# Six early output stores issued by ScalarE, SyncE's loads in the order of use, and two stretches of attention moved up by 14 products

## The chip, the cores and the metric

The kernel runs on one core of a Trainium2 chip. Times are device microseconds (us) of one execution, given as the median of several with the range; most executions of one kernel agree within 0.3%. A difference counts as faster or slower where it is over 2%.

## The reference, cut to what matters

```python
# q, k, v: (8 batches, 8 heads, 576 positions, 64)   all float32
scores = q @ k^T / 8
ret    = scores * Dmat            # Dmat[h,i,j] = gamma_h ** (i-j) for i >= j, else 0
x      = (ret @ v) as (4608 tokens, 512)
out    = ((x @ w_a) * (x @ w_b)) @ w_out      # 512 -> 1536 -> 512
```

A retention (attention without a softmax, whose decay allows running states) feeds a gated feed-forward network. Nearly all arithmetic is in the three products of the network.

## The kernel before

The 4608 tokens are handled as 18 pairs of 128. TensorE runs the network block by block: 512 tokens, 256, 256, then 512 each. Between its products stand the pieces of attention for later tokens. The first six 128-row steps use small pieces (transposing on TensorE, scores, states, outputs); from pair 3 on a whole pair is done in one "stretch" whose transposed queries and keys come from DMA transposes.

SyncE issues the loads, the transposes and the stores, all in one list, in the order of the program text as the build's scheduler lays it out:

```python
def load_pair(n, which=(0, 1, 2)):          # q, k, v of one pair, two issues each
    paired.setdefault(n, [])
    for i in which:
        ...
        for kp, r0, m, b, s0 in rows_of(n):
            nc.sync.dma_start(t[...], src[b, :, s0:s0 + m, :]...)
        paired[n].append(t)

def turn(n):                                 # q and k of a pair, transposed by DMA
    for w in (0, 1):
        nc.sync.dma_start_transpose(qkT[:, w]..., qkb[:, w])

def store(u, cols, osb):                     # one 128-token output tile
    ...
    if n < FIRST:                            # FIRST = 3: the first six tiles
        for par in (0, 1):                   # their tokens are interleaved: two half stores
            nc.sync.dma_start(rows[par::2], osb[half(par), cols])
    else:
        nc.sync.dma_start(rows, osb[r0:r0 + m, cols])
```

ScalarE and VectorE evict. Three of ScalarE's copies matter here: the transposed queries of the small steps, the running states, and `ha`, the first of the two activations, which frees one of four PSUM buffers:

```python
COPY["act"](qkT[:, w], tp...)               # line 318, before score_step
nc.scalar.copy(ha[:, 0:n], pa[:, 0:n])      # line 690, once per 128 columns of w_a
...
if (u + part) % 2 == 0:                      # an output tile leaves PSUM
    nc.scalar.copy(osb[:, cols], po[:, 0:width])
else:
    nc.vector.tensor_copy(osb[:, cols], po[:, 0:width])
store(tok0 // 128 + u, cols, osb)            # osb has four buffers
```

A table says at which count of products each piece is laid into the stream:

```python
todo += [(170, stretch, (3, None)), (197, stretch, (4, 3)),
         (246, stretch, (5, 4)), (280, stretch, (6, 5)), ...]
casts = {3: 104, 4: 104.1, 5: 143, 6: 200, 7: 250, 8: 330}
turns = {4: 104.2, 5: 151, 6: 210, 7: 338, 8: 345}
loads = {7: 212, 8: 271, 9: 345.1, 10: 345.2}
```

`stretch(6, 5)` scores pair 6 and finishes pair 5. Synchronization is not written by hand: the framework gives each transfer of SyncE and ScalarE one of eight completion counters in turn, and makes the issuer wait until the previous user of that counter has landed.

## Time and profile before

| | before |
|---|---|
| median time (4 runs) | 333.47 us (332.73 to 334.26) |
| span of the profiled execution | 331.8 us |
| TensorE busy | 319.8 us, with 36 of its 3648 matmul records missing |
| ScalarE busy | 128.6 us (39%) |
| mean granted TensorE clock | 1.00 |

The prediction below shows the page's busy times, the chain, the waits and the time line; they are not repeated. Two rows from the table of windows of before serve for comparison later. They give, for each stretch of time, every engine's busy microseconds, then the granted clock, the mean share of the DMA engines that is busy, and the traffic.

```profile
core 0: us, PE busy (x) PEld busy (x) DVE busy (x) ACT busy (x) POOL busy (x), PEclk, DMA share, GB/s
40.00:60.00 20.00, 19.63 (x221) 12.61 (x223) 9.49 (x17) 8.63 (x22) 14.83 (x20) 1.00 1.04 225
60.00:80.00 20.00, 18.47 (x322) 14.13 (x322) 12.94 (x29) 9.66 (x24) 10.12 (x12) 1.00 1.08 205
```

TensorE has work for 38.1 of these 40 us, ScalarE for 18.3, and the DMA engines are full.

One reading needs care. Before's list of waits has ten of 0.16 us each at the output products and six at the first products "until issue". They are 1.6 and 1.0 us, and I take them for missing records: runs 9 and 10 below, which also have 3612 matmul records, have the same entries, and the kernels with all 3648 have not. So TensorE's true busy time is about 319.8 + 2.6 = 322.4 us (an estimate), to be used when it is compared with kernels whose records are complete.

### The profile page before, as it was taken

What the parts mean: (1) busy time and instruction counts of PE and PEld (TensorE: products, weight loads), DVE (VectorE), ACT (ScalarE), POOL (GpSimd) and SP (SyncE); (2) the same over time, 40 slices, a digit from 0 to 9 for tenths busy, and PEclk for the clock granted to TensorE, in tenths of its full rate; (3) what the DMA queues carried; (4) which work ended last, traced back from release to release, by engine and by line L of the source; (5) the groups of instructions that cost most, each with busy time, mean ns of one, the idle gap of its engine ahead of it and who ended that gap; (6) DMA issues with size and microseconds to landing.
All of it is one profiled execution on the core that took longest, in us unless ns stands there. A gap on an engine that the chain in (4) does not pass through costs nothing.

```text
span 331.8 us, 8671 instructions
## 1 busy us (share of the span) xinstructions
PE 319.8 (96%) x3612; PEld 168.1 (51%) x3648; DVE 163.7 (49%) x292; ACT 128.6 (39%) x275; POOL 114.6 (35%) x146
## 2 busy tenths in 40 slices
PE   8999999989989999999999999999999999999996
PEld 4644456848634554545454545454445444444443
DVE  5734435664674465656265625662456246414321
ACT  7734744553543344343235313532332333213321
POOL 4870078835277274634063405360430000000000
DMA  8999999999999998992599258945850420031013
GB/s 220 248 172 208 236 227 222 225 166 234 199 205 254 214 215 200 206 219 54 140 224 213 61 127 188 224 71 149 180 116 4 138 54 0 2 95 34 1 26 100
DMA packets 143175, 50.37 MB, mean 152 GB/s; under 512 B 124576, under 2 KB 138656, under 8 KB 143136
## 3 DMA queue, kind: packets, MB, share of 16 engines
q1 hardware_dynamic: 138384, 45.10, 65.0%
q0 software_dynamic: 4752, 4.72, 8.7%
q8 instruction: 28, 0.46, 0.6%
q14 instruction: 11, 0.09, 0.1%
HBM read 37.75 MB, written 9.44 MB: 142 GB/s over the span
## 4 chain that ended last, share of the span: by engine, by line
PE 86%; DMA 5%; SPq 2%; issue 2%; DVE 2%; ACT 1%; POOL 1%; DVEq 0%; POOLq 0%; ACTq 0%
PE po L716 27%; PE pb L697 27%; PE pa L682 26%; SPq L153 2%; DMA vf<-in_v_dram 2%; DMA qf<-in_q_dram 2%; PE o L589 2%; PE o L602 1%; DMA qkT<-qkb 1%; PE sc L563 1%; PE kv L506 1%; PE kv L359 1%; DVE sums L526 0%; POOL qkb L440 0%; PE pa L664 0%
## 5 line engine op out<-in xcount | busy, mean ns | idle before, releaser
L702 DVE TENSOR_TENSOR hT<-ha,pb 128x512 bf16<-128x512 bf16 (+1 forms) x120 | 75.8, 633 | 99.6 <-PE pb L697 95.2
L690 ACT CAST ha<-pa 128x512 bf16<-128x512 f32 (+1 forms) x120 | 64.8, 543 | 122.7 <-PE pa L682 121.5
L697 PE MATMUL pb<-xT,wb_sb 128*128 128x512 bf16 (+1 forms) x474 | 111.5, 357 | 0.4
L682 PE MATMUL pa<-xT,wa_sb 128*128 128x512 bf16 (+1 forms) x459 | 108.4, 357 | 2.8 <-DVE xT L612 1.4
L716 PE MATMUL po<-wo_sb,hT 128*128 128x512 bf16 (+1 forms) x430 | 95.0, 373 | 1.8 <-issue 1.6
L697 PEld LDWEIGHTS <-wb_sb 128*128 128x128 bf16 x480 | 46.8, 98 | 46.4 <-issue 0.3
L682 PEld LDWEIGHTS <-wa_sb 128*128 128x128 bf16 x474 | 45.5, 98 | 46.7 <-issue 1.9
L716 PEld LDWEIGHTS <-hT 128*128 128x128 bf16 x444 | 42.3, 98 | 46.8
L440 POOL CAST qkb<-qf 64x1024 bf16<-64x1024 f32 x15 | 15.4, 1029 | 85.8 <-DMA qf<-in_q_dram 85.0
L445 POOL TENSOR_TENSOR vb<-vf,vs 128x1024 bf16<-128x1024 f32 x15 | 28.5, 1901 | 12.4 <-DMA vf<-in_v_dram 6.3
L727 DVE COPY osb<-po 128x512 f32<-128x512 f32 (+1 forms) x18 | 12.2, 676 | 40.7 <-PE po L716 40.7
L725 ACT COPY osb<-po 128x512 f32<-128x512 f32 (+1 forms) x19 | 10.9, 574 | 44.4 <-PE po L716 41.5
L526 DVE TENSOR_TENSOR sums<-kv,sums 128x256 f32<-128x256 f32 x46 | 19.5, 423 | 2.8 <-PE kv L506 0.8
L612 DVE TENSOR_TENSOR xT<-o,qs 128x512 bf16<-128x512 f32 x30 | 19.6, 682 | 2.5 <-PE o L602 2.5
L572 DVE TENSOR_TENSOR sT<-sc,mask 128x512 bf16<-128x512 f32 x30 | 19.4, 680 | 0.0
L444 POOL CAST qkb<-kf 64x512 bf16<-64x512 f32 x30 | 17.6, 614 | 0.9
L444 POOL CAST qkb<-qf 64x512 bf16<-64x512 f32 x30 | 17.6, 614 | 0.7
L440 POOL CAST qkb<-kf 64x1024 bf16<-64x1024 f32 x15 | 15.5, 1033 | 4.2 <-DMA kf<-in_k_dram 3.2
L530 ACT CAST states<-sums 64x512 bf16<-64x512 f32 x26 | 16.0, 617 | 0.3
L299 POOL CAST qkb<-kf 128x512 bf16<-128x512 f32 x5 | 3.1, 613 | 20.0 <-DMA kf<-in_k_dram 20.0
L740 PE MATMUL w<-ones 128*128 128x256 bf16 (+1 forms) x36 | 8.3, 359 | 1.5 <-DVE ones L197 1.5
L563 PE MATMUL sc<-qkT 64*64 64x64 bf16 x480 | 7.4, 195 | 1.3 <-DMA qkT<-qkb 1.3
(81 smaller groups left out, 155.7 us busy)
## 6 DMA issues: line engine op xcount, KB each, us to landing
qf<-in_q_dram SPq DMA_DIRECT2D x32, 256.0 KB, 4.5
kf<-in_k_dram SPq DMA_DIRECT2D x32, 256.0 KB, 5.1
vf<-in_v_dram SPq DMA_DIRECT2D x32, 256.0 KB, 5.1
out_dram<-osb SPq DMA_DIRECT2D x25, 256.0 KB, 2.2
out_dram<-osb SPq DMA_DIRECT2D x22, 128.0 KB, 2.4
wo_sb<-in_moe_w_out_dram POOLq DMA_DIRECT2D x3, 512.0 KB, 18.0
qf<-in_q_dram SPq DMA_DIRECT2D x8, 128.0 KB, 3.2
kf<-in_k_dram SPq DMA_DIRECT2D x8, 128.0 KB, 3.5
```

What stands on the lines that cost most here:

```text
L440: nc.gpsimd.tensor_copy(qkb[0:64, w], t[0:64])
L444: nc.gpsimd.tensor_copy(to[:, :, 1 - r], fro[:, :, r])
L445: nc.gpsimd.tensor_tensor(vb.rearrange("p (k h d) -> p k h d", k=2, h=H), vf.rearrange("p (k h d) -> p k h d", k=2, h=H), vs2[:, 2 if n in ...
L526: nc.vector.tensor_tensor(sums[:, i], own, prev, op=ALU.add)
L530: nc.scalar.copy(to(half(1 - r)), fro(half(r)))
L572: nc.vector.tensor_tensor(sT[:, on].rearrange("p c k s -> p (c k) s"), sc[:, on].rearrange("p c k s -> p (c k) s"), mask3.unsqueeze(1).to_ ...
L612: nc.vector.tensor_tensor(x_of(t0, 128).rearrange("p c (a s) -> p c a s", a=2), o[:, :, :, kp].rearrange("p a c s -> p c a s"), qs[:, :, s ...
L682: nc.tensor.matmul(pa[:, 0:n], wa_sb[:, c, fs], xT[:, c], start=(c == 0), stop=(c == NC - 1))
L690: nc.scalar.copy(ha[:, 0:n], pa[:, 0:n])
L697: nc.tensor.matmul(pb[:, 0:n], wb_sb[:, c, fs], xT[:, c], start=(c == 0), stop=(c == NC - 1))
L702: nc.vector.tensor_tensor(hT[:, F, 0:n], has[F][:, 0:n], pb[:, 0:n], op=ALU.mult)
L716: nc.tensor.matmul(po[:, 0:width], hT[:, F, u * 128:(u + 1) * 128], wo_sb[:, F, cols], start=(F == 0), stop=(F == NF - 1))
```

## The change

The intent: the first output tile is ready at 43 us, and its store stands in SyncE's list behind loads that move at the pace of the transfers. Let ScalarE issue the first six tiles' stores; close up SyncE's loads and transposes for pairs 4 to 7 in the order of use; with the transposes earlier, lay two stretches 14 products earlier so that their results are there before the next block wants them. (The 14 is the table's count, and a piece is laid in at the next edge of a group of products: in the traces the first stretch moves up by 32 products of half the width, that is 16, and the second by 12.) In the 256-token blocks both output tiles are evicted by ScalarE, so that the issuer of the store is also the engine that made the tile.

```diff
             if n < FIRST:
                 for par in (0, 1):
-                    nc.sync.dma_start(rows[par::2], osb[half(par), cols])
+                    nc.scalar.dma_start(rows[par::2], osb[half(par), cols])
...
-                if (u + part) % 2 == 0:
+                if n == 256 or (u + part) % 2 == 0:
                     nc.scalar.copy(osb[:, cols], po[:, 0:width])
...
-    for n in range(FIRST, FIRST + 3):
+    for n in (FIRST, FIRST + 1):
         load_pair(n)
+    load_pair(FIRST + 2, (Q, K))
...
-             (246, stretch, (5, 4)), (280, stretch, (6, 5)),
+             (232, stretch, (5, 4)), (266, stretch, (6, 5)),
...
-    casts = {3: 104, 4: 104.1, 5: 143, 6: 200, 7: 250, 8: 330}
-    turns = {4: 104.2, 5: 151, 6: 210, 7: 338, 8: 345}
-    loads = {7: 212, 8: 271, 9: 345.1, 10: 345.2}
-    todo += [(150, load_pair, (6, (0, 1))), (152, load_pair, (6, (2,)))]
+    casts = {3: 104, 4: 104.1, 5: 141, 6: 200, 7: 250, 8: 330}
+    turns = {4: 104.2, 5: 142, 6: 213, 7: 338, 8: 345}
+    loads = {7: 146, 8: 271, 9: 345.1, 10: 345.2}
+    todo += [(104.3, load_pair, (5, (V,))), (104.4, load_pair, (6, (K,))),
+             (112.2, load_pair, (6, (Q,))), (112.4, load_pair, (6, (V,)))]
```

Cut from the diff: `paired[n]` becomes a dictionary, so that single tensors of a pair can be loaded at different places.

More of the change, by code (lines that the diff above doesn't have):

```diff
@@ L136, in load_pair @@
             return
-        paired.setdefault(n, [])
+        paired.setdefault(n, {})
         for i in which:
@@ L145, in load_pair @@
                     src[b, :, s0:s0 + m, :].rearrange("h s d -> s h d"))
-            paired[n].append(t)
+            paired[n][i] = t
     def load_step(n, hh, which):
@@ L433, in ahead @@
     def ahead(n):
-        qf, kf, vf = paired.pop(n)
+        qf, kf, vf = (paired[n].pop(i) for i in (Q, K, V))
         qkb = nat.tile([128, 2, 2 * DM], BF16, tag="qkb", name="qkb2")
```

## The prediction

> **What bounds the kernel now.** I read the page's first and fourth parts, then the waits of TensorE, then the time line of TensorE, ScalarE and SyncE between 34 and 76 us, where all the moved instructions stand.
>
> ```profile
> PE 319.8 (96%) x3612; PEld 168.1 (51%) x3648; DVE 163.7 (49%) x292; ACT 128.6 (39%) x275; POOL 114.6 (35%) x146
> PE 86%; DMA 5%; SPq 2%; issue 2%; DVE 2%; ACT 1%; POOL 1%; DVEq 0%; POOLq 0%; ACTq 0%
> PE pa L682 <- DVE xT L612: 1.4, 1, 1.4
> PE sc L563 <- DMA qkT<-qkb: 1.3, 1, 1.3
> ```
>
> TensorE sets the end: 96% busy, 86% of the chain. Its list of waits has only two that this change can remove: 1.3 us for the transposed pair 4 (at 70 us) and 1.4 us for the last activations of the fourth token block (at 95 us). With the small holes that lengthen four product groups between 82.7 and 86.8 us to 4.1 us from some 3.5, the whole prize is 3.3 us, 1%.
>
> Next, SyncE, whose rows are start, length, what it issues:
>
> ```profile
> 34.91 0.65 SPq L806 DMA_DIRECT2D gate<-wo_sb  x1
> ...
> 45.81 2.75 SPq L142 DMA_DIRECT2D vf<-in_v_dram x2
> 48.68 2.35 SPq L142 DMA_DIRECT2D qf<-in_q_dram x2
> ...
> 55.20 2.29 SPq L142 DMA_DIRECT2D qf<-in_q_dram x2
> 57.59 3.38 SPq L142 DMA_DIRECT2D kf<-in_k_dram x2
> 61.07 1.87 SPq L142 DMA_DIRECT2D vf<-in_v_dram x2
> 63.04 1.46 SPq L653 DMA_DIRECT2D out_dram<-osb x2
> 64.60 3.28 SPq L471 DMA_TRANSPOSE qkT<-qkb x2
> 67.97 3.88 SPq L653 DMA_DIRECT2D out_dram<-osb x6
> ```
>
> SyncE is held at a gate until the output weights have landed (34.9 us); then it issues loads back to back, about 1.15 us for each 256 KB, which is the 220 to 227 GB/s of the page's slices there: it goes at the pace of the transfers. So the first store leaves at 63.0 us. Against that, the engines:
>
> ```profile
> 42.58 0.59 ACT L725 COPY osb<-po 128x512 f32<-128x512 f32 x1 [0.38 <-PE po L716]
> 43.67 0.59 ACT L318 COPY qkT<-tp 128x512 bf16<-128x512 bf16 x1 [0.50 <-PE tp L316]
> 44.65 0.42 PE L331 MATMUL sc<-qkT 64*64 64x128 bf16 x16
> 48.63 0.42 PE L331 MATMUL sc<-qkT 64*64 64x128 bf16 x16
> ```
>
> The first output tile is ready at 43.2 us and waits 20 us in SyncE's queue. Right behind it ScalarE copies the transposed queries that TensorE needs at 44.65 us.
>
> **What the Trainium skill says.** "DMA: Bandwidth & Descriptors", section "Issuing engines are not separate DMA queues": transfers issued by SyncE and ScalarE share the same 16 DMA engines, and issuing from two saves only issue time. The trace agrees so far that one queue moves 65% of 16 engines' time and the loads are paced by transfer. "Perfetto Trace Analysis", section "DMA Instruction — HWDGE (DVE, Sync)": the sequencer itself sits in the semaphore wait before such an issue, and the profiler's row starts after it. The trace has such a case: the gate's row starts at 34.91 us, and none of the loads listed behind it, which wait for nothing that the weights give, goes before it. The trace of before has no DMA on ScalarE; that ScalarE's queue blocks alike is my inference.
>
> **The change, part by part.** (1) Twelve half stores (six tiles, two issues each) leave SyncE's list and stand in ScalarE's. In the trace eight of them take 546 to 819 ns each, median 597, to issue: 12 x 0.6 = 7.2 us of ScalarE, which is 39% busy; by itself nearly hidden. (2) In the two 256-token blocks both output evictions go to ScalarE: two more copies of 0.59 us, two fewer of 0.69 on VectorE. Hidden. (3) SyncE's loads and transposes for pairs 4 to 7 close up by the eight half stores' 5.3 us or so; transposed pair 4 is there long before its use. (4) Two stretches stand 14 products earlier. TensorE's work is the same in number (7298 rows in both programs).
>
> But the built program says what a store waits for, beside its tile. All transfers of SyncE and ScalarE take eight completion counters in turn, in one common order, and each waits for the one before it on its counter. In that common order the stores are interleaved with loads that SyncE has not reached in reality, since the gate and the transfers hold it back. ScalarE works strictly down its list, so it will stand at the store until that load has landed, and the query copy behind it stands too. I walk down the six tiles, with issue times and landing times from the trace of before (SyncE's list is unchanged up to the k of pair 5):
>
> Tile 1, first half: waits for the second half of pair 3's v, issued 46.65, landed 5.8 us later: 52.4. Second half: second half of pair 4's q, issued 49.5 + 4.7 = 54.2. Issue 0.7, query copy 0.6: TensorE's first score step moves from 44.65 to 55.5, +10.9.
> Tile 2: second half of pair 5's q (56.2 + 6.1 = 62.3), then first half of its k (57.6 + 5.6 = 63.2). Issue 0.7, copy 0.6: the second score step moves from 48.63 to 64.5, +15.9. The work between the two steps, 4 us, disappears inside this wait.
> Tile 3: second transpose of pair 4, then first half of pair 5's v. SyncE is through with k at 61.0, transposes take 1.4 + 1.8, so v leaves at 64.2 and lands a median 4.7 later: 68.9. Issue 0.7, state copy 0.5: the second output step moves from 52.74 to 70.1, +17.4.
> Tile 4: first half of pair 6's q, four loads of 1.1 us behind that v: 68.6 + 4.7 = 73.3. Issue 0.7, copy of a 0.4: TensorE, which has four PSUM buffers for products and so runs two product pairs ahead, gets its third at 74.4 instead of 55.91, +18.5.
> Tile 5 (block 1, first half): first k and v of pair 7; by then SyncE is ahead: no wait.
> Tile 6: second transpose of pair 6, then q of pair 8. That transpose waits for TensorE to have read pair 3's queries (its first stretch with states, 68.6 before, so 87.1). Two transposes 3.2 (90.3), q lands 4.5 later (94.8), issue and copy 1.0: 95.8 for the third product of block 2, 75.99 before. Without this wait it would come at 75.99 + 18.5 - 1.3 (the wait for pair 4, now gone) = 93.2; so 2.6 more, +19.8.
>
> From there TensorE is dense (192.1 of the 195 us from 105 to 300 us busy, by the windows), so the delay runs through to the end. The moved stretch takes back 1.4: +18.4. The stores that now go out between 52 and 73 us take 0.6 us of transfer each (128 KB at 220 GB/s) from the loads that the gates wait for; I estimate 1 us of it on the path. Sum +19.4: 333.0 + 19.4 = 352.4 us; I say 352.
>
> **Rivals.** First, the intent: stores issue at once, the two waits go, 330 us. For it: part 3 is right by itself. Against it: it needs 52.4 and 62.3 us landings to have happened at 43 and 47 us. Second, only the issue cost shows: ScalarE loses 7.2 us in pieces of 1.3, and some product evictions come late by one piece, 331 to 335. Against it: the same. Third, the waits as worked out and besides a slow TensorE after each long hole: at the start its first eight 128x512 products take 3.59 us, whereas sixteen take 3.62 at 39.8 us, so after idling it runs at half speed for some 4 us. After the first hole this lies in the second's shadow; after the second it can add up to 2, later ones are short: 354 to 357. Fourth, the gates give way earlier, because transfers are less crowded while everything stands still (5.8 us landings shrink to 4): each gate 1 to 2 us sooner, 347 to 349.
>
> **Range and chances.** The first two gates (+15.9) rest on landings that the change doesn't touch; gates 3, 4 and 6 add 1 to 6. So 345 to 358 should hold it 8 times in 10. Faster by over 2% would take more than the whole prize: 0.02. Within 2%: 0.07, if the counters turn out not to hold ScalarE. Slower: 0.91.
>
> **What would show it.** In the changed kernel's profile ScalarE idles 9 us before its first store and some 5 before the third and fourth half stores; TensorE has two holes, about 11 and 5 us, before score steps, ended by ScalarE's query copy, and its total busy time is the same or a few us more. First half stores leave at 52 and 62 us, not 43 and 47. The waits for pair 4's transposes and for the last xT are gone. The page's load on DMA slackens between 75 and 100 us. I am wrong if ScalarE's first store leaves at 43 us, if TensorE's holes are short while the span grows by a slower TensorE or later waits after 100 us, or if the loads before the gates land at other times.

## The result, and the profile after

The changed kernel takes 352.29 us (351.62 to 352.89, 4 runs) against 333.47 us. The ratio is 1.0563, with a 95% interval from 1.0526 to 1.06: slower. In the profiled execution the span is 350.1 us against 331.8.

The page of the changed kernel, its busy times, its row of the granted clock in 40 slices (before's page has no such row; its mean granted clock is 1.00) and its chain:

```profile
PE 325.9 (93%) x3648; PEld 168.8 (48%) x3648; DVE 162.3 (46%) x290; ACT 129.0 (37%) x277; POOL 114.7 (33%) x146
PEclk9999976999999999999999999999999999999999
PE 75%; DMA 11%; SPq 7%; POOL 4%; issue 1%; DVE 1%; ACT 1%; ACTq 0%; POOLq 0%; DVEq 0%
```

DMA has come into the chain with 11% where it had 5%, and SyncE's queue with 7% where it had 2%. ScalarE itself is no busier: 129.0 us against 128.6. The list of TensorE's waits says where the time went (microseconds in total, times, longest):

```profile
PE sc L331 <- ACT qkT L318: 12.6, 2, 9.8
PE pa L682 <- ACT ha L690: 3.1, 2, 1.9
PE o L400 <- ACT state_after L372: 1.8, 1, 1.8
```

These three are its longest, and each is for a ScalarE copy (next comes 1.5 us at the start of the program, which before has too). The two that the change was to remove (pair 4's transposes, the fourth block's activations) are gone. ScalarE is not slow in these copies; it is late. Its own time line shows why. A row with ACTq is an issue by ScalarE, x2 meaning the two half stores of one tile; the brackets give the idle time before a copy, and what ended it:

```profile
51.04 2.80 ACTq L653 DMA_DIRECT2D out_dram<-osb  x2
53.88 0.59 ACT L318 COPY qkT<-tp 128x512 bf16<-128x512 bf16 x1 [10.71 <-DMA out_dram<-osb]
...
60.53 1.73 ACTq L653 DMA_DIRECT2D out_dram<-osb  x2
62.29 0.59 ACT L318 COPY qkT<-tp 128x512 bf16<-128x512 bf16 x1 [7.31 <-DMA kf<-in_k_dram]
...
66.23 2.19 ACTq L653 DMA_DIRECT2D out_dram<-osb  x2
68.46 0.53 ACT L372 CAST state_after<-kv 64x128 bf16<-64x128 f32 x2 [3.52 <-DMA vf<-in_v_dram]
...
71.41 2.45 ACTq L653 DMA_DIRECT2D out_dram<-osb  x2
73.90 0.65 ACT L690 CAST ha<-pa 128x256 bf16<-128x256 f32 x2 [4.28 <-DMA out_dram<-osb]
```

ScalarE stood idle for 10.71 us before the query copy at 53.88 us; the profile names a store as what ended the wait in two rows, a load of k and a load of v in the others. A query copy has nothing to do with a load of pair 5's k: only the store in front of it has, through the counter. The half stores' issue times, next to the landing of the transfer that used the same counter before (from the trace's completion records), agree as follows.

| half store | issued, us | previous transfer on its counter | landed, us |
|---|---|---|---|
| tile 1, first | 51.04 | pair 3's v, second half | 50.96 |
| tile 1, second | 53.36 | pair 4's q, second half | 53.34 |
| tile 2, first | 60.53 | pair 5's q, second half | 60.45 |
| tile 2, second | 61.65 | pair 5's k, first half | 61.62 |
| tile 3, first | 66.23 | pair 4's transposes, second | 66.15 |
| tile 3, second | 67.94 | pair 5's v, first half | 67.92 |
| tile 4, second | 73.38 | pair 6's q, first half | 73.36 |
| tile 6, second | 94.59 | pair 8's q, first half | 94.57 |

Eight half stores leave 0.02 to 0.08 us after that landing. Four are not in the table: the first halves of tiles 4 and 6, which went when their tile or turn came, and tile 5's two, which did not wait for a landing. The completion records of runs 1, 5 and 9 below, which also issue early stores from ScalarE, have fourteen more half stores that leave 0.02 to 0.08 us after such a landing.

TensorE's rows, with the idle time before each in brackets:

```profile
54.52 0.64 PE L331 MATMUL sc<-qkT 64*64 64x128 bf16 x16 [9.80 <-ACT qkT L318]
55.09 3.23 PE L716 MATMUL po<-wo_sb,hT 128*128 128x512 bf16 x8
...
62.93 0.42 PE L331 MATMUL sc<-qkT 64*64 64x128 bf16 x16 [2.81 <-ACT qkT L318]
...
69.05 0.28 PE L400 MATMUL o<-qkT,state_after 128*128 128x128 bf16 x2 [1.84 <-ACT state_after L372]
...
74.32 0.60 PE L682 MATMUL pa<-xT,wa_sb 128*128 128x256 bf16 x4 [1.93 <-ACT ha L690]
...
95.53 0.60 PE L682 MATMUL pa<-xT,wa_sb 128*128 128x256 bf16 x4 [1.17 <-ACT ha L690]
```

These are the gates of the prediction's sum, in order. Before, they stood at 44.65, 48.63, 52.74, 55.91 and 75.99 us. The eight products behind the first hole took 3.23 us; before, eight of them took 1.90. The two windows that correspond to those of before:

```profile
40.00:60.00 20.00, 10.20 (x80) 4.97 (x78) 3.45 (x5) 2.84 (x6) 15.83 (x20) 0.74 1.17 239
60.00:80.00 20.00, 13.42 (x204) 9.53 (x201) 7.05 (x15) 6.13 (x17) 6.76 (x8) 1.00 1.17 225
```

In these 40 us TensorE's busy time falls from 38.1 to 23.6 us and ScalarE's from 18.3 to 9.0, while the DMA engines stay full. The clock granted from 40 to 60 us is 0.74 instead of 1.00.

In the profile the loss divides into idle and slow time. Of the 18.3 us of span, TensorE's busy time accounts for 325.9 - 322.4 = 3.5 us and its idle time for the other 14.8. That does not make 3.5 us a separate cause: the slow products after the first hole ran while ScalarE stood at the second one, so they filled idle time that was there anyway.

### The profile page after: what moved, and what is told of

It is laid out like the page before. It is cut to its first block, busy times and chain, and to the rows that moved or that the text cites. A ratio compares the mean times of both kernels' runs of the same rounds, so it can differ in the third digit from the quotient of the medians.

```text
span 350.1 us, 8705 instructions
## 1 busy us (share of the span) xinstructions
PE 325.9 (93%) x3648; PEld 168.8 (48%) x3648; DVE 162.3 (46%) x290; ACT 129.0 (37%) x277; POOL 114.7 (33%) x146
## 4 chain that ended last, share of the span: by engine, by line
PE 75%; DMA 11%; SPq 7%; POOL 4%; issue 1%; DVE 1%; ACT 1%; ACTq 0%; POOLq 0%; DVEq 0%
PE pa L682 23%; PE po L716 23%; PE pb L697 23%; DMA wo_sb<-in_moe_w_out_dram 4%; DMA vf<-in_v_dram 3%; DMA qf<-in_q_dram 3%; SPq L153 3%; SPq L142 2%; SPq L471 2%; PE o L589 2%; PE o L602 1%; PE sc L563 1%; PE kv L506 1%; POOL vb L309 1%; DMA out_dram<-osb 1%
## 5 line engine op out<-in xcount | busy, mean ns | idle before, releaser
L682 PE MATMUL pa<-xT,wa_sb 128*128 128x512 bf16 (+1 forms) x474 | 110.3, 358 | 3.1 <-ACT ha L690 3.1
L716 PE MATMUL po<-wo_sb,hT 128*128 128x512 bf16 (+1 forms) x444 | 99.0, 377 | 0.1
L727 DVE COPY osb<-po 128x512 f32<-128x512 f32 (+1 forms) x16 | 10.8, 675 | 40.5 <-PE po L716 40.5
L725 ACT COPY osb<-po 128x512 f32<-128x512 f32 (+1 forms) x21 | 12.1, 575 | 46.9 <-PE po L716 46.9
L526 DVE TENSOR_TENSOR sums<-kv,sums 128x256 f32<-128x256 f32 x46 | 19.5, 423 | 2.8 <-PE kv L506 0.8
L612 DVE TENSOR_TENSOR xT<-o,qs 128x512 bf16<-128x512 f32 x30 | 19.5, 683 | 2.2 <-PE o L602 2.2
L572 DVE TENSOR_TENSOR sT<-sc,mask 128x512 bf16<-128x512 f32 x30 | 19.5, 682 | 0.0
L331 PE MATMUL sc<-qkT 64*64 64x128 bf16 x96 | 2.7, 236 | 12.8 <-ACT qkT L318 12.6
L339 DVE TENSOR_TENSOR sT<-sc,mask_s 128x1024 bf16<-128x1024 f32 x6 | 7.3, 1222 | 11.9 <-PE sc L331 11.8
L318 ACT COPY qkT<-tp 128x512 bf16<-128x512 bf16 x6 | 3.5, 586 | 19.4 <-DMA out_dram<-osb 10.7
```

Source lines behind the costliest of these rows:

```text
L526: nc.vector.tensor_tensor(sums[:, i], own, prev, op=ALU.add)
L572: nc.vector.tensor_tensor(sT[:, on].rearrange("p c k s -> p (c k) s"), sc[:, on].rearrange("p c k s -> p (c k) s"), mask3.unsqueeze(1).to_ ...
L612: nc.vector.tensor_tensor(x_of(t0, 128).rearrange("p c (a s) -> p c a s", a=2), o[:, :, :, kp].rearrange("p a c s -> p c a s"), qs[:, :, s ...
L682: nc.tensor.matmul(pa[:, 0:n], wa_sb[:, c, fs], xT[:, c], start=(c == 0), stop=(c == NC - 1))
L716: nc.tensor.matmul(po[:, 0:width], hT[:, F, u * 128:(u + 1) * 128], wo_sb[:, F, cols], start=(F == 0), stop=(F == NF - 1))
```

## The experiments

Theory: ScalarE stands at its stores until unrelated loads have landed, and its copies behind the stores come late; everything else in the change moves the time by 3 us at most, downwards. Rivals: the issue cost of the stores on ScalarE, the traffic of the early stores, and the moved transposes and stretches themselves. Eleven kernels were run, all with correct results.

| kernel | time, us (range, runs) | before, us | ratio (95% interval) |
|---|---|---|---|
| stores to ScalarE only | 356.64 (355.43 to 357.88, 4) | 334.23 | 1.0676 (1.0633 to 1.0719) |
| all but the stores | 343.68 (339.51 to 344.31, 6) | 334.23 | 1.026 (1.0213 to 1.0308) |
| all, stores on GpSimd | 339.10 (338.48 to 342.12, 6) | 334.23 | 1.0175 (1.0132 to 1.0218) |
| twelve later stores on ScalarE | 333.54 (333.27 to 333.84, 6) | 334.23 | 0.9985 (0.9957 to 1.0013) |
| first tile's store on ScalarE only | 343.84 (343.28 to 344.31, 4) | 333.48 | 1.031 (1.0284 to 1.0336) |
| before, stores on GpSimd | 337.11 (334.51 to 337.60, 8) | 333.48 | 1.0112 (1.0089 to 1.0134) |
| the same, stretches moved | 337.07 (334.24 to 338.76, 6) | 333.48 | 1.0103 (1.0068 to 1.0138) |
| before, stretches moved only | 338.24 (336.38 to 340.74, 6) | 333.48 | 1.0144 (1.0108 to 1.0181) |
| changed, stretches put back | 352.05 (351.66 to 353.92, 5) | 333.88 | 1.0559 (1.0534 to 1.0583) |
| before, pair 4 transposed first | 334.05 (333.44 to 335.51, 6) | 333.88 | 1.0009 (0.9988 to 1.0031) |
| the same, one stretch moved by 8 | 335.30 (333.79 to 338.40, 6) | 333.88 | 1.0046 (1.001 to 1.0083) |

By the 2% rule the first, second, fifth and ninth are slower, the third is unclear (its interval reaches over 2%), and the others are the same. Where an interval lies clear of 1 the text below still speaks of a loss, of 0.5 to 1.8%; it is measured, but small.

### 1. Only the stores move to ScalarE

```diff
-                    nc.sync.dma_start(rows[par::2], osb[half(par), cols])
+                    nc.scalar.dma_start(rows[par::2], osb[half(par), cols])
```

> The kernel before with one word changed: the twelve half stores of the first six tiles are issued by ScalarE; SyncE's loads, transposes and the stretches stay as before. Counter theory (each store takes the counter of a load eight places back in a common order in which SyncE stands ahead of where it really is): 350 to 356 us; first half store leaves at 51 to 53 us, TensorE has holes of about 10 and 3 to 6 us before its score steps, ended by ScalarE's query copy. Rival, issue cost alone: 332 to 336 us, first half store at 43 us. Rival, the loss comes from the reordered loads or the moved stretches: 333 us here.

It took 356.64 us, slightly above the range: this one word by itself costs more than the whole change. Its waits are of the same kind, 14.4 us at the score steps instead of 12.6 and 3.7 at the products instead of 3.1; the 1.8 us before the output step is not there, and the 1.4 us for the fourth block's activations has stayed. The larger part of the surplus is elsewhere. Its span is 6.0 us longer than the changed kernel's (356.1 against 350.1), and its TensorE is busy 5.0 us longer (330.9 against 325.9) with the same number of matmuls, at a mean granted clock of 0.966 instead of 0.985. Output products after its second hole, in the time line of TensorE:

```profile
67.06 1.89 PE L716 MATMUL po<-wo_sb,hT 128*128 128x512 bf16 x4
69.67 1.89 PE L716 MATMUL po<-wo_sb,hT 128*128 128x512 bf16 x4
71.97 1.04 PE L716 MATMUL po<-wo_sb,hT 128*128 128x512 bf16 x4
```

Twice four products take 1.89 us, then four take 1.04. Here the slow clock lies behind the second hole, where no further hold of ScalarE hides it. The later wait of 3.12 us at the last gate (98.73 us) does not hide it either: it ends with a load that stood behind pair 6's transposes, and these left at 89.59 us, just after TensorE had read pair 3's queries (89.43). So the prediction's third rival happened in this kernel, and not in the profiled execution of the changed one.

### 2. Everything but the stores

The changed kernel with this line put back:

```diff
-                    nc.scalar.dma_start(rows[par::2], osb[half(par), cols])
+                    nc.sync.dma_start(rows[par::2], osb[half(par), cols])
```

> The changed kernel with its twelve half stores back on SyncE: the new order of loads and transposes, both evictions of the 256-token blocks on ScalarE and the two moved stretches remain. Counter theory: all of the 19 us is gone; 331 to 336 us. The waits for pair 4's transposes (1.3) and for the last xT (1.4) are gone; but stores 2 to 4 now stand behind four loads more, so the second tile's output buffer comes free only near 77 us, which may give 3 to 4 us back as a wait of ScalarE's output copy. Rival, the loss comes from the reordered loads or the moved stretches: 345 us or more.

It took 343.68 us where at most 336 was expected: a miss. No copy of queries is held, so the holes of the changed kernel are gone. In their place stand three others, the first row from ScalarE's time line and the rest from TensorE's:

```profile
76.80 0.59 ACT L725 COPY osb<-po 128x512 f32<-128x512 f32 x1 [3.86 <-DMA out_dram<-osb]
```

```profile
82.14 0.44 PE L563 MATMUL sc<-qkT 64*64 64x64 bf16 x32 [1.73 <-DMA qkT<-qkb]
96.26 0.64 PE L563 MATMUL sc<-qkT 64*64 64x64 bf16 x32 [4.10 <-DMA qkT<-qkb]
```

An output copy waits for one of the four output buffers, whose store now stands behind the transposes and loads laid ahead of it; TensorE loses 3.2 us by that. The two stretches laid earlier wait 1.73 and 4.10 us for the transposes of pairs 5 and 6. So the theory that the rest of the change is harmless falls. It is harmless only in the company of the stores: in the changed kernel the holes keep TensorE back by 16 to 19 us, while SyncE and its transfers go on, and the same transposes are in time: pair 5's landed at 80.09 us and were used at 97.88, pair 6's at 92.60 and 107.81.

### 3. Everything, with the stores on GpSimd

```diff
-                    nc.scalar.dma_start(rows[par::2], osb[half(par), cols])
+                    nc.gpsimd.dma_start(rows[par::2], osb[half(par), cols])
```

GpSimd's transfers use other counters than those of SyncE and ScalarE, in the built program.

> The changed kernel with its twelve half stores issued by GpSimd, whose transfers take counters of their own (last used by the weight loads, which landed by 40 us). Counter theory: no store waits for a load, the first leaves when GpSimd is through with pair 3's values (about 55 us), ScalarE never stands; 329.5 to 332 us, faster than before by up to 1%. Rival, an early store disturbs the loads by its traffic and this is what costs: still 345 or more, since the stores go out as early as in the changed kernel. Rival, GpSimd gets late by standing at stores: a few us, 332 to 336, with waits for GpSimd's casts on TensorE's list.

It took 339.10 us: 13 us less than the changed kernel, but nowhere near the 329.5 to 332 that was expected. As expected, ScalarE never stands: its longest idle times between 44 and 75 us end with a result of TensorE. But TensorE waits twice for transposes, first for pair 4's and then for pair 5's. The first of these rows is SyncE's, the others are TensorE's:

```profile
60.51 4.26 SPq L471 DMA_TRANSPOSE qkT<-qkb  x2
```

```profile
70.08 0.44 PE L563 MATMUL sc<-qkT 64*64 64x64 bf16 x32 [1.54 <-DMA qkT<-qkb]
82.56 0.64 PE L563 MATMUL sc<-qkT 64*64 64x64 bf16 x32 [4.10 <-DMA qkT<-qkb]
```

Issued 4 us earlier than before, pair 4's second transpose landed at 70.04 us, as late as before's at 70.10. GpSimd had issued six half stores at 61.0 to 64.2 us, just as the transposes went out.

### 4. Twelve half stores on ScalarE, later

In the kernel before, the six tiles of pairs 12 to 14 are stored by twelve half stores from ScalarE, where the transfers ahead on the counters have long landed:

```diff
+            elif 12 <= n <= 14:
+                for p0 in (0, 64):
+                    nc.scalar.dma_start(rows[p0:p0 + 64],
+                                        osb[p0:p0 + 64, cols])
             else:
                 nc.sync.dma_start(rows, osb[r0:r0 + m, cols])
```

> The kernel before, with six later tiles (pairs 12 to 14, after 200 us, where SyncE waits for tiles and is not behind) stored by twelve half stores of ScalarE, as many as in the change. Counter theory: their counters belong to transfers that landed long ago, ScalarE stands nowhere for long; the same time as before within 0.3% (332 to 334.5). Rival, ScalarE's issue cost by itself delays product evictions: 336 to 341 us.

It took 333.54 us, ratio 0.9985. Twelve issues by ScalarE cost nothing that can be seen. This removes the rival that the issue cost is what is paid.

### 5. One tile

```diff
-                    nc.sync.dma_start(rows[par::2], osb[half(par), cols])
+                    queue = nc.scalar if (n, u) == (0, 0) else nc.sync
+                    queue.dma_start(rows[par::2], osb[half(par), cols])
```

> The kernel before with only the first tile's two half stores issued by ScalarE. Counter theory: one hold, until pair 4's q has landed near 53.3 us; TensorE has one hole of about 9.8 us before the first score step and none before the second; of it the 1.3 us wait for pair 4's transposes is saved, so 340 to 343 us. Rival, the holds come from ScalarE's queue as such (a slow first issue[...]): then the hole has nothing to do with 53.3 us, and the issue ends at a time of its own.

It took 343.84 us, within the range: two issues of 0.55 and 0.49 us cost 10.4 us. TensorE's time line has the one hole, and its second score step no wait:

```profile
54.38 0.64 PE L331 MATMUL sc<-qkT 64*64 64x128 bf16 x16 [9.99 <-ACT qkT L318]
```

This is the first gate alone, at 54.38 us where the whole change has it at 54.52. It also shows that the gates are not to be added up: the second one is worth what it comes later than the first, and so on.

### 6. The kernel before, with the stores on GpSimd

```diff
-                    nc.sync.dma_start(rows[par::2], osb[half(par), cols])
+                    nc.gpsimd.dma_start(rows[par::2], osb[half(par), cols])
```

> The kernel before with the twelve half stores issued by GpSimd, order of loads, transposes and stretches as before. Order theory (the run with GpSimd stores in the changed order was 1.75% slower because pair 5's transposes stand behind five more loads there, while the stretch that needs them was moved up): here pair 5's transposes land near 76 us instead of 82.5, the wait for pair 4's (1.3) is gone; 331 to 332.5 us. Rival, GpSimd's stores themselves disturb: 335 us or more.

337.11 us: early stores without any hold of ScalarE make the kernel 1.1% slower, where a gain had been expected. The profiled execution was the fastest of the eight (334.51 us), so it understates this; the seven slower ones, which were not profiled, were granted 0.990 to 0.995 of the clock, this one 1.00. GpSimd's issues, SyncE's transposes of pair 4 and TensorE's wait for them, each from its own engine's time line:

```profile
61.06 3.17 POOL L653 DMA_DIRECT2D out_dram<-osb  x6
```

```profile
63.14 6.14 SPq L471 DMA_TRANSPOSE qkT<-qkb  x2
```

```profile
71.38 0.45 PE L563 MATMUL sc<-qkT 64*64 64x64 bf16 x32 [2.69 <-DMA qkT<-qkb]
```

The two transposes leave 1.5 us earlier than before (63.14 against 64.60), as the change intended, but issuing them takes 6.14 us instead of 3.28. They have landed by 71.34 us instead of 70.10, and TensorE's wait has grown from 1.32 to 2.69 us. The stores are the only transfers that are new there. That their traffic is what stretches the issue of the transposes fits runs 3 and 6, but no run took the traffic away by itself, and not all of it can be theirs: in run 10 the transposes left as early (62.99 us) with no store beside them, and issuing them took 4.45 us.

### 7. The same, with the two stretches moved

```diff
-             (246, stretch, (5, 4)), (280, stretch, (6, 5)),
+             (232, stretch, (5, 4)), (266, stretch, (6, 5)),
```

> The same as the run with GpSimd stores in the order of before, and the two stretches moved up by 14 products. Order theory: pair 5's transposes (near 76 us) are there before the moved stretch needs them (78.3), pair 6's too (82 against 88); both waits of the kernel before are gone: 329.5 to 331.5 us, 0.6 to 1% faster than before. Rival, the moved stretches cost by themselves: 335 or more.

337.07 us, as run 6, and again a miss. With pair 5's transposes at 78.8 us and pair 6's at 84.8, no later stretch waits for transposes, and the fourth block's activations are in time. The 1.4 us so gained are lost at another place: 2.58 us before an output product, at 93.78 us, for which the profile shows no releaser. Run 8 has the same hole, and what it is stands there.

### 8. Only the stretches moved

The same edit in the kernel before, with the stores on SyncE.

> The kernel before with the two stretches moved up by 14 products and nothing else. Order theory: the stretch needs pair 5's transposes at about 78 us, they land at 81.4, so a wait of 3 us comes and the 1.4 us wait for the last xT goes: 333.5 to 336 us. Rival, no wait since the transposes come first: 332.

338.24 us, over the upper end of the range. In TensorE's time line:

```profile
82.14 0.45 PE L563 MATMUL sc<-qkT 64*64 64x64 bf16 x32 [3.44 <-DMA qkT<-qkb]
...
95.94 3.41 PE L716 MATMUL po<-wo_sb,hT 128*128 128x512 bf16 x15 [1.99 <-issue]
```

The first of these could have been read from the trace of before. There pair 5's transposes had landed at 81.43 us, and TensorE used them at 81.84: a margin of 0.4 us. The stretch now comes 16 products of 0.216 us, or 3.5 us, earlier, so it has to wait about 3.0 us there (an estimate); with the transposes landing 0.67 us later, at 82.10, it waited 3.44. Pair 6's margin was 2.4 us (landed 88.60, used 90.96). The second hole is the one of run 7, at the same product; the built program has no wait for a semaphore there.

The traces do tell what it is. Among a trace's DMA packets are 28 of 16 KB that carry instructions ("q8 instruction: 28" on every page), one for each 256 of TensorE's 7316 rows. In the kernels with complete records, each hole of over 0.3 us without a releaser (the first 5 us of the program left out) stands before a row whose number is 193 more than a multiple of 256: row 2497 in runs 3 (0.5 us, at 96.92), 7 and 8, row 1729 in the changed kernel (0.4 us, at 88.06), and row 449 in run 7 (0.4 us, at 16.13). Each ends 1.40 to 1.47 us after such a packet has landed, in run 8 the one of 93.17 to 94.47 us. And at none of these rows, in any of the nine complete traces, does TensorE start less than 1.3 us after its packet. So TensorE stood for its next block of instructions, while the DMA engines were full (a share of 1.14 in run 7 and 1.28 in run 8, in the 4 us around the hole). This is read from times alone; no run changed it. Why the packet came late in these two is not shown: it started 2.3 and 1.7 us after TensorE had entered the block before, in run 3, with the same move, 0.2.

### 9. The changed kernel, with the stretches put back

```diff
-             (232, stretch, (5, 4)), (266, stretch, (6, 5)),
+             (246, stretch, (5, 4)), (280, stretch, (6, 5)),
```

> The change, with the two stretches put back 14 products later. My sum credited the moved stretches with 1.4 us, so it expects 353.5 to 354 us here against 352.3 for the whole change, and the 1.4 us wait for the last activations of the fourth block back at about 124 us. The rival that the runs so far suggest: with 16 to 19 us of holds before them the transposes are there early at either place, so both places cost the same on that side, and the move itself brings only what the wait is worth or nothing: 352 to 353.

352.05 us (ratio 1.0559) against the changed kernel's 352.29 (1.0563). The wait for the fourth block's activations is back, though smaller and earlier than expected:

```profile
115.25 1.02 PE L682 MATMUL pa<-xT,wa_sb 128*128 128x512 bf16 x4 [0.76 <-DVE xT L612]
```

The intervals overlap nearly wholly: moving the stretches gains nothing measurable in the changed kernel. The difference is uncertain by some 1.5 us (an estimate from the two intervals), so the times alone do not rule the credited 1.4 us out; but the wait that the move takes away is 0.76 us long here. The profiled execution of this run was its slowest of five (353.92 us), so the two spans are not compared: behind the last gate, at 95.66 us, four products of half the width took 1.01 us instead of 0.60, the third rival once more.

### 10. Pair 4 transposed ahead of the first store

```diff
-    casts = {3: 104, 4: 104.1, 5: 143, ...}
-    turns = {4: 104.2, 5: 151, ...}
+    casts = {3: 103.8, 4: 103.9, 5: 143, ...}
+    turns = {4: 104.0, 5: 151, ...}
```

> Before, with one change: the casts and the transposes of pair 4 are placed one step earlier, so that the transposes stand ahead of the first tile's store in SyncE's list. If the waits behind late transposes are what the free part of the change can win or lose, the 1.3 us wait at 70 us goes and the time is 331.7 to 332.5 us against 333.5. If something else has the time there (the copies of the same pair, the products' PSUM buffers), it stays at 333.3 to 333.7.

334.05 us, the same as before. TensorE's rows:

```profile
69.63 0.45 PE L563 MATMUL sc<-qkT 64*64 64x64 bf16 x32 [0.83 <-DMA qkT<-qkb]
...
82.56 0.45 PE L563 MATMUL sc<-qkT 64*64 64x64 bf16 x32 [1.05 <-DMA qkT<-qkb]
```

The wait for pair 4 fell by 0.5 us only, since the transposes landed at 69.59 instead of 70.10, although they left 1.6 us earlier: issuing them took 4.45 us instead of 3.28. TensorE, earlier by 0.5 us, then overran the small margin of pair 5 and waited 1.05 us there. The total was 1.9 us of waiting for transposes where before had 1.3.

### 11. The same, and one stretch moved by 8 products

```diff
-             (246, stretch, (5, 4)), (280, stretch, (6, 5)),
+             (246, stretch, (5, 4)), (270, stretch, (6, 5)),
```

> The same, and the second moved stretch placed 8 products earlier than before instead of 14, the first one left where it was. Pair 6's transposes landed at 88.6 us in before and would be needed at about 89.2, pair 5's are not touched. If landing times decide, the 1.4 us wait for the last activations goes as well: 330.3 to 331.5 us. If an earlier place of this stretch brings a hole of its own, as the 2 us hole with no releaser in the two kernels with the 14-product move, it is 332 to 334.

335.30 us, above both outcomes (332 to 334 for the second). The table's 10 come to 8 products in the trace. The 1.4 us wait for activations is gone. But in this execution SyncE left its gate, the wait for the output weights, at 35.80 us (before: 34.91), and the stretch at 71.47 us waits 2.0 us. The profile puts this down to VectorE's sums; yet the instruction that waits names the counter of pair 4's second transpose, which landed at 71.43 us, so it is the old wait for transposes, longer. At 93.83 us there is 0.67 us of the hole of runs 7 and 8, ended 1.35 us after an instruction packet had landed. No version that beats the kernel before was found.

## Why the prediction was right, and where it was not

The predicted time was 352 us and the measured 352.29. The sum was +19.4 us on a before of 333.0; measured are +18.8 on 333.47, and +18.3 between the profiled executions. The gates, as predicted and as TensorE's time line has them:

| gate | predicted, us | measured, us | predicted shift | measured shift |
|---|---|---|---|---|
| first score step | 55.5 | 54.52 | +10.9 | +9.9 |
| second score step | 64.5 | 62.93 | +15.9 | +14.3 |
| second output step | 70.1 | 69.05 | +17.4 | +16.3 |
| third product, block 1 | 74.4 | 74.32 | +18.5 | +18.4 |
| third product, block 2 | 95.8 | 95.53 | +19.8 | +19.5 |
| end of the span | | | +19.4 | +18.3 |

**The counters hold ScalarE: right, and shown.** The issue times coincide with the landings (table above), one tile alone brings the first gate (run 5), the same stores later cost nothing (run 4), and on GpSimd's counters ScalarE is not held (run 3). That ScalarE's queue blocks in its wait like SyncE's had been an inference; it is measured now.

**The walk down the gates: right within 1.6 us.** The first three came 1.0, 1.6 and 1.1 us sooner than worked out, because those loads landed earlier than in before: pair 4's q at 53.34 instead of 54.22, pair 5's first k at 61.62 instead of 63.23. For the first gate that is not the fourth rival's reason. The load took 5.00 us to land instead of 4.69, but SyncE had left its gate at 33.80 us instead of 34.91, before anything that the change moved; over all the profiled executions this moment lies between 33.1 and 35.8 us, so about 1 us either way is chance. At the second gate shorter transfers come in too (that k took 4.78 us instead of 5.64), as the fourth rival had it. The fourth gate came as computed by two errors that cancel: pair 6's q left 0.9 us earlier than worked out (67.67 instead of 68.6) and took 1.0 us longer (5.69 instead of 4.7). The last came as computed step by step: transposes at 87.11 us for 87.1, the load landed at 94.57 for 94.8. Tile 5 waited for nothing, also as computed.

**The signs.** First half stores were expected at 52 and 62 us and left at 51.04 and 60.53. Holes of about 11 and 5 us were expected before the score steps; they are 9.80 and 2.81. The second is short because TensorE's work between the two steps took 5.6 us instead of 4, at the slow clock, in the shadow of the hold as the third rival said. One sign was wrong: the load on the DMA engines was to slacken between 75 and 100 us. Until 100 us it did so only from 85 to 90 (0.75), and it stopped from 100 to 110 (0.00 and 0.01).

**Issue cost and evictions hidden: right for the issue** (run 4). The evictions moved to ScalarE were not tested by themselves; ScalarE's busy time is 129.0 us against 128.6, and TensorE's list has 0.5 us, at 93.77, for one of these copies. It lies before the last gate, which the load of pair 8's q sets.

**Transposed pair 4 "is there long before its use": right in the changed kernel only.** It landed at 66.15 us and was used at 87.09, because its use had been put off by 17 us (70.14 before). Where its use was not put off it came at 70.04 (run 3), 71.34 (run 6) and 69.59 us (run 10), against 70.10 before.

**The moved stretch "takes back 1.4": not confirmed.** In the changed kernel's trace the wait is gone, and the shift falls from +19.5 at the last gate to +18.3 at the end. But the wait is only 0.76 us long in the kernel with the stretches put back, which is no slower in the timed runs (run 9), and without the holes the move costs 1.4% (run 8). The step forgot to ask when pair 5's and pair 6's transposes land.

**One microsecond for the stores' traffic: neither shown nor refuted.** The shift at the last gate was +19.5 without it, against +19.8 predicted. The load that sets the fourth gate did take 1.0 us longer than assumed, with stores in flight beside it; but in before, without such stores, the loads of those microseconds took anything from 4.7 to 6.1 us, and no run separates this. Traffic is a plausible cost in runs 3 and 6, which have no holes.

These last two terms, +1.0 and -1.4, are the ones that no run confirms. They nearly cancel, and the first is estimated at a size that the spread of the runs (1.3 us) hides; so the closeness of the total, 352.0 against 352.29, says less for them than for the gates, and part of it is luck.

**The rivals.** The intent, 330 us, is refuted, and more than by the holds: the rest of the change costs 2.6% without them (run 2), and even with the stores on an engine that is not held it costs 1.75% (run 3). Part 3 was not "right by itself", as the prediction said in its favour. The issue cost alone is refuted by runs 4 and 5. The slow TensorE exists in the changed kernel, but in the profiled execution it lies within a wait; where it lies outside one, it was paid (runs 1 and 9). Three gates did give way earlier by 1.0 to 1.6 us, though the first for another reason than this rival's, and the last, which sets the end, did not.

Two parts that cost 6.8% and 2.6% alone cost 5.6% together. That is why a part of a change should not be called harmless from the trace of the whole: here the holds hid the waits of the rest.

What stays open: why TensorE's instructions came late in runs 7 and 8; the share of the stores' traffic in the later transposes; and 3.1 us of run 2's 9.4: its three holes (1.73, 4.10 and 3.22 us, less before's 1.3 and 1.4) name 6.3, in a profiled execution that was 2.2 us faster than the median. Its slow clock is part of the answer: its TensorE is busy for 325.0 us, 2.6 more than before's estimated 322.4, and its four slower executions were granted 0.984 to 0.985 of the clock, the two faster 0.993.

## What to carry to other kernels

Before moving a transfer to another engine, ask not what its issue costs but what it will wait for, in the built program: a completion counter used in turn ties it to a transfer that has nothing to do with it, and everything behind it on that engine is tied as well. An idle engine is a good issuer only if its list holds nothing urgent behind the issue, or if the transfers ahead on the counters have landed by then. And before laying work earlier, look up the landing time of each of its inputs: a use without a wait may have a margin of 0.4 us. Where a profile names no releaser, look among the DMA packets too: TensorE's own instructions came through them.

## What the Trainium skill lacked or had wrong

- "DMA: Bandwidth & Descriptors", section "Issuing engines are not separate DMA queues", says that issuing on several engines saves only the sequencer's time. It does not say what it can cost: two issues of 0.5 us on a second engine made the kernel 10.4 us slower (run 5), since in this program the issuer stands until the previous transfer on the counter has landed. The same issues where nothing is outstanding cost nothing (run 4).
- "TensorE: Matmul & The Clock Gate", section "What's actually happening", puts an idle array at half rate. This case agrees (eight products in 3.23 us after a 9.80 us hole, and in 3.60 after one of 10.07 in run 1, where before takes 1.90), and adds that the loss need not reach the end: it did not where the next hold covered it, and four products took 1.89 instead of 1.04 us, twice, where nothing did (run 1).
- No page tells what stores in flight do to DMA transposes: issuing two took 6.14 us beside six half stores (run 6), 4.45 as early without them (run 10) and 3.28 in before.
- No page gives a size for what TensorE loses when its next block of instructions comes late: 2.58 and 1.99 us between two products of one group, with no wait in the program and no releaser in the profile (runs 7 and 8).
